# Loading the queries in rows of 2 KB, eight tokens of one head per partition

## The chip, the cores and the metric

The kernel runs on one core of one Trainium2 chip. The metric is the device time of one execution in microseconds (us). The engines are named as in the profile: PE (TensorE matmul) and PEld (its weight loads), DVE (VectorE), ACT (ScalarE), POOL (GpSimd) and SP (SyncE, which issues nearly all DMAs here). A name with a q behind it (SPq, ACTq) is the engine's instruction queue, where DMAs are issued.

## What is computed

Two layers in a row, over B = 4 batches, 768 tokens, 8 heads of 64. First linear attention with a decay per head, in blocks of 64 tokens; then a gated layer whose gate mixes over tokens.

```python
for b in range(nb):                       # 12 blocks of 64 tokens
    intra = einsum('bhic,bhjc->bhij', qb, kb) * Dmask      # lam**(i-j) for i >= j, else 0
    intra = einsum('bhij,bhjd->bhid', intra, vb)
    inter = einsum('bhid,bhde->bhie', qb * lam_pow, kv_state)
    out[:, :, sl] = intra + inter
    kv_state = lam_block * kv_state + einsum('bhsd,bhse->bhde', kb * rev_pow, vb)
x = out as (B, S, H*D)
h = maximum(x @ w_in, 0)
u, v = halves of h;  v_n = (v - mean) / sqrt(var + 1e-6)
v_s = einsum('ts,bsd->btd', w_spatial, v_n) + b_spatial
return (u * v_s) @ w_out
```

## The kernel before

The kernel does not leave the order of its work to a scheduler. The string `ORDER` lists some 700 tokens such as `QM.0.1.D`: a step, its arguments, and the engine that does it (T for PE, D for DVE, A for ACT, P for POOL, S for SP). A loop at the end of the kernel issues each step to its engine in that order. So each engine executes its own tokens strictly in the order of the list, and an instruction that waits holds up all that stand behind it on that engine. Steps of different engines meet only through the data and the buffers that they share.

The attention is done in 12 steps n, three of 256 tokens for each batch. For a step, SP loads k, q and v (`LK`, `LQ`, `LV`, 512 KB each, three buffers of each kind) with 512 bytes in a row: partition p holds the tokens 2p and 2p+1 of all eight heads. `KM` and `QM` (function `decay`, L331; half of the heads in one instruction) multiply k and q by powers of lam, taken from the tables `lv` and `lqn`, into the bf16 tiles `kc` and `qc`. `TK` and `TQ` (L366) transpose these on PE, `EK` and `EQ` evict the transposes into `kT` and `qT`; for some later steps `DK` and `DQ`, transposes by DMA, do the same. `SC` (L396) multiplies them into scores, `MK` (L401) applies the 0/1 mask `m01`, `KP` (L425) builds the state, `AV` adds the state's part (L459) and the block's own part (L468), and `EX` evicts the attention's result, transposed, into `xT`. `VC` and `VD` cast v to bf16.

The second layer follows in the same list: `PV` and `BN` (L493, L508), `PU` (L544), `WT` (transposes of the spatial weights), `PW` (L570), `GP`, `GM` (L576), `PO` (L581), and `ST`, the stores. Weights are loaded by SP (`WH`, `WQ`, `WP`) and cast to bf16 by `CW`, `CX`, `WC`, `WX`.

What matters around the change is the start. Before the first `KM` the two tables must exist. lam is loaded by ACT's queue (`lam`, L200); PE spreads it over 128 partitions by a matmul with a row of ones (`LB`, L216); ACT takes the logarithm (`LN`, L219); DVE multiplies it by the token's position (`LL`, L222, positions from POOL's `posk`, L203 and L204); ACT takes two exponentials (`LX`, L226 and L227), one for each table. Until lam is there, PE executes 13 filler matmuls of a tile of ones (`FL`, L309), which DVE has set to one in its first instruction (`one`, L305). More fillers stand at fixed places in the first third of the list. The start of the list:

```
LK.0.S LQ.0.S LQ.1.S LK.1.S LV.0.S LQ.2.S BR.A lam.A tab.0.A msk.P idn.P posk.P one.D row.D FL.2.256.0.1.T
```

POOL's own first steps are `msk` (L233, L234), `idn` (the identity for transposes), `posk`, and then `QM.1.0` and `QM.1.1`, the query decays of step 1, and `KM.1.0`, `KM.1.1`. DVE's first large steps are `KM.0.0`, `QM.0.0`, `QM.0.1`, `KM.0.1`.

Of the kernel before, what the change touches and what calls it, by code (L numbers as in the profile page):

```python
# [16 lines left out]
LK.0.S LQ.0.S LQ.1.S LK.1.S LV.0.S LQ.2.S BR.A lam.A tab.0.A msk.P idn.P posk.P one.D row.D FL.2.256.0.1.T  # L17
FL.2.256.5.1.T FL.2.256.3.1.T FL.2.256.4.1.T FL.2.256.1.1.T FL.1.256.3.1.T FL.2.256.5.1.T LB.1.T LN.1.A eps.D mkc.D
LL.D LX.A KM.0.0.D QM.0.0.D QM.0.1.D KM.0.1.D FL.1.256.6.1.T BB.1.2.T BB.0.0.T TQ.0.0.3.T FL.2.256.1.1.T TK.0.0.6.T
tab.1.A BE.1.2.A VC.0.A TQ.0.1.4.T TK.0.1.5.T EQ.0.0.3.D EK.0.0.6.D EQ.0.1.4.D EK.0.1.5.D BE.0.0.D FL.1.256.1.1.T  # L20
SC.0.0.2.3.T QM.1.0.P QM.1.1.P KM.1.0.P KM.1.1.P SC.0.1.5.6.T MK.0.0.2.3.D MK.0.1.5.6.D QM.2.1.D FL.2.256.1.1.T
TQ.1.0.1.T FL.4.256.4.1.T TK.1.0.0.T TK.1.1.3.T TQ.1.1.5.T KP.0.2.T AV.0.0.6.4.T QM.2.0.P LK.2.S KM.2.1.P KM.2.0.P
LV.1.S WH.0.S WH.1.S LV.2.S LQ.3.S WH.3.S VD.1.1.P CW.2.P EQ.1.0.1.D SX.0.D EQ.1.1.5.A SY.0.2.A EK.1.1.3.A
FN.0.6.4.D EK.1.0.0.D TQ.2.1.5.T AV.0.1.6.4.T SA.0.1.D EQ.2.1.5.D SC.1.0.1.2.T EX.0.0.6.A EX.0.1.4.A FL.2.256.0.1.T
FL.1.256.3.1.T TQ.2.0.0.T SC.1.1.5.6.T TK.2.1.4.T FL.2.256.3.1.T FL.1.256.3.1.T FL.1.256.3.1.T TK.2.0.3.T
MK.1.0.1.2.D MK.1.1.5.6.D EQ.2.0.0.A VD.1.0.A EK.2.1.4.A KP.1.2.T AV.1.0.0.1.T SY.1.2.D SA.1.0.D FN.1.0.1.D
EK.2.0.3.A SC.2.1.4.5.T FL.1.256.6.1.T CW.0.A CW.1.A SC.2.0.2.3.T AV.1.1.0.1.T WQ.0.S WQ.1.S WQ.2.S WH.2.S WC.0.P
WC.1.P WC.2.P MK.2.1.4.5.D MK.2.0.2.3.D SA.1.1.D VC.2.D CW.3.A EX.1.1.1.A EX.1.0.0.A PV.0.1.6.T PV.0.0.4.T
PV.1.0.5.T KP.2.6.T AV.2.0.2.3.T SA.2.0.D EV.0.1.6.A FN.2.2.3.A EV.0.0.4.A GP.0.0.0.1.A PV.1.1.6.T FL.1.256.0.1.T
AV.2.1.2.3.T EX.2.0.2.A QM.3.1.D QM.3.0.D TQ.3.2.4.T CX.1.D PU.0.1.0.T PU.1.1.2.T EX.2.1.3.A EV.1.1.6.A BN.0.0.D  # L30
EV.1.0.5.A BN.0.1.D RA.0.A EU.0.1.0.A EU.1.1.2.A PV.2.0.3.T PV.2.1.6.T BN.1.1.D BN.1.0.D EV.2.0.3.A RA.1.A
EV.2.1.6.A WT.0.0.3.T WT.2.0.5.T EW.2.0.5.A PU.2.1.2.T WT.1.0.0.T BN.2.0.D RD.1.D BN.2.1.D VN.1.1.D RD.0.D RB.0.D
EW.0.0.3.A RA.2.A VN.0.0.A CX.0.P PU.2.0.6.T EU.2.0.6.A VN.0.1.A EW.1.0.0.D RD.2.D LK.3.S PU.1.0.5.T PU.0.0.3.T
VN.2.0.D VN.1.0.D VN.2.1.D LK.4.S WQ.3.S EU.1.0.5.D GP.0.2.0.6.D EU.2.1.2.A GP.0.1.0.5.A EU.0.0.3.A GP.0.3.0.2.A
KM.3.0.P WQ.4.S WQ.5.S LV.3.S LQ.4.S LQ.5.S LV.4.S KM.4.0.P QM.4.0.P QM.4.1.P QM.5.0.P QM.5.1.P VC.4.P PW.0.0.0.1.T
KM.4.1.D KM.3.1.D WC.3.D GM.0.0.0.1.D PW.0.1.0.5.T PW.0.2.0.6.T TK.3.2.0.T WC.4.A EQ.3.2.4.A EK.3.2.0.A WC.5.D
GM.0.1.0.5.D GM.0.2.0.6.D WT.2.1.3.T WT.0.1.1.T EW.0.1.1.D WP.S VC.3.D EW.2.1.3.A GP.0.1.1.6.A PW.0.3.0.2.T
WT.1.1.4.T LK.5.S GM.0.3.0.2.D SC.3.1.0.1.T KP.3.5.T SC.3.0.2.3.T MK.3.1.0.1.D EW.1.1.4.A PW.0.1.1.6.T TK.4.2.0.T
MK.3.0.2.3.D GP.0.3.1.1.A GP.0.2.1.2.A SY.3.5.A PW.0.3.1.1.T SA.3.1.D SX.3.D GM.0.1.1.6.D GP.0.0.1.3.A TQ.4.2.4.T
PW.0.2.1.2.T GM.0.2.1.2.D GM.0.3.1.1.D PW.0.0.1.3.T GM.0.0.1.3.D EK.4.2.0.A EQ.4.2.4.A KM.5.0.P KM.5.1.P  # L40
AV.3.0.5.6.T SC.4.0.1.2.T KP.4.0.T FN.3.5.6.A AV.3.1.5.6.T SY.4.0.D SC.4.1.3.4.T EX.3.1.6.A TQ.5.2.0.T WX.0.A WX.1.A
EX.3.0.5.D MK.4.0.1.2.D SA.4.1.D MK.4.1.3.4.D SA.4.0.D LV.5.S PV.3.1.6.T PU.3.1.5.T PO.0.1.1.T PO.0.3.2.T TK.5.2.4.T
PV.3.0.3.T LV.6.S LK.6.S EK.5.2.4.D EO.0.1.1.A EQ.5.2.0.A EV.3.1.6.A EU.3.1.5.A EO.0.3.2.D VC.5.P AV.4.0.6.0.T
# [45 lines left out]
def kernel(  # L89
# [37 lines left out]
    ps = psum.tile([P, 8, 512], FP32, name="ps")  # L127
    SB = 7

    lam_in = sb([1, H], FP32, "lam_in")  # L130
    one_row = sb([1, P], FP32, "one_row")
    loglam = sb([P, H], FP32, "loglam")
    ident = sb([P, P], BF16, "ident")
# [186 lines left out]
    def ld_q(e, n):  # L320
        load(q, q_in, n, e)
# [322 lines left out]
```

## Time and profile before

| | |
|---|---|
| time, median of 2 executions | 143.69 us (143.64 to 143.75) |
| the profiled execution: its time, its span | 144.71 us, 143.0 us |
| PE, DVE, ACT, POOL busy, share of the span | 94%, 81%, 58%, 36% |
| granted TensorE clock, mean | 0.972 |
| moved by DMA | 33.60 MB, 235 GB/s over the span |

The page of the profile gives the busy time of each engine, the span in 40 slices, the chain of work that ended last, and the costliest groups of instructions. The timeline lists instructions by start and duration, merged where like ones follow each other ("x2"); a bracket at the end of a row tells how long the engine was idle before and what released it. The windows give the busy time of each engine in a stretch of the span, the clock that TensorE was granted, and the bytes per second of the DMAs. A row is read as: start, duration, engine, line of the kernel, operation, written tile <- read tiles, shapes.

### The profile page before, as it was taken

Reading aid. Unit: us, or ns where it says so; the run is one execution under the profiler, and the core shown is the slowest. Engines: PE = TensorE matmul, PEld = TensorE weight load, DVE = VectorE, ACT = ScalarE, POOL = GpSimd, SP = SyncE. Lnnn points to the kernel's source line nnn. Section 1 sums busy time; section 2 is a strip of 40 time slices with the busy share of each in tenths; the row PEclk is TensorE's granted clock in tenths of the full one; section 3 lists DMA queues with packets and bytes.
Section 4 is the critical chain, followed back from the end, with each engine's and each line's share of the span. In section 5 each row is a group of like instructions: output and inputs, shape, how many; then the busy total and the mean of one; then the engine's idle time right before and its main releaser. Section 6 shows DMA issues by size and latency. Waiting matters only on the chain.

```text
span 143.0 us, 4741 instructions
## 1 busy us (share of the span) xinstructions
PE 133.8 (94%) x1999; PEld 87.7 (61%) x2014; DVE 115.3 (81%) x236; ACT 82.8 (58%) x158; POOL 51.9 (36%) x61
## 2 busy tenths in 40 slices
PE   5969999899999899999999999999999999999990
PEld 4448774676666667567666565676665665666630
DVE  3399798989997769699399988995798889874760
ACT  3422895798978577569611586689113627791121
POOL 5077710555095343991770006920822000000000
PEclk9975899999999999999999999999999999999998
DMA  3999999899999899959904799998994403930284
GB/s 87 347 347 346 386 323 315 294 339 313 337 302 344 259 288 324 285 166 290 293 0 78 49 282 354 180 142 238 276 257 126 177 5 117 406 139 0 78 324 185
DMA packets 54617, 33.60 MB, mean 235 GB/s; under 512 B 11715, under 2 KB 49859, under 8 KB 54596
## 3 DMA queue, kind: packets, MB, share of 16 engines
q1 hardware_dynamic: 54448, 33.17, 80.7%
q8 instruction: 15, 0.25, 0.7%
q10 hardware_dynamic: 148, 0.13, 0.3%
q14 instruction: 6, 0.05, 0.1%
HBM read 24.38 MB, written 6.29 MB: 215 GB/s over the span
## 4 chain that ended last, share of the span: by engine, by line
PE 83%; DVE 9%; ACT 3%; issue 2%; DVEq 0%; ACTq 0%
PE ps L570 21%; PE ps L581 14%; PE ps L493 13%; PE ps L544 11%; PE ps L396 5%; PE ps L366 5%; PE ps L309 4%; PE ps L468 4%; PE ps L425 3%; PE ps L459 2%; DVE st L508 2%; DVE qc L331 2%; DVE kc L331 2%; DVE vn L532 1%; DVE win_sb L183 1%
## 5 line engine op out<-in xcount | busy, mean ns | idle before, releaser
L570 PE MATMUL ps<-wt_sb,vn 128*128 128x384 bf16 x192 | 33.7, 326 | 0.5 <-ACT vn L529 0.3
L331 POOL TENSOR_TENSOR kc<-k_in,lv 128x512 bf16<-128x512 f32 x20 | 20.5, 1043 | 30.0 <-PE ps L493 11.5
L401 DVE TENSOR_TENSOR a_sb<-ps,m 128x1024 bf16<-128x1024 f32 x24 | 28.4, 1211 | 0.7 <-PE ps L425 0.6
L570 PEld LDWEIGHTS <-vn 128*128 128x128 bf16 x192 | 18.3, 98 | 12.3 <-ACT vn L529 0.6
L544 PE MATMUL ps<-xT,win_sb 128*128 128x256 bf16 x192 | 23.6, 273 | 0.5 <-DVE win_sb L183 0.5
L331 POOL TENSOR_TENSOR qc<-q_in,lqn 128x512 bf16<-128x512 f32 x18 | 19.3, 1090 | 10.2 <-DMA q_in<-in_q_dram 5.2
L493 PE MATMUL ps<-win_sb,xT 128*128 128x512 bf16 x89 | 22.3, 379 | 0.4
L581 PE MATMUL ps<-wout_sb,gT 128*128 128x512 bf16 x84 | 22.1, 379 | 0.4
L576 DVE TENSOR_TENSOR gT<-ps,uT 128x384 bf16<-128x384 f32 x32 | 16.8, 551 | 7.1 <-PE ps L570 6.7
L544 PEld LDWEIGHTS <-win_sb 128*128 128x128 bf16 x192 | 18.4, 98 | 5.1 <-DVE win_sb L183 0.7
L181 ACT ACTIVATE ps<-bsp 128x384 f32<-128x384 f32 x23 | 11.2, 490 | 10.7 <-DVE gT L576 6.7
L508 DVE BATCH_NORM_STATS2 st<-vh 128x6 f32<-128x512 bf16 x24 | 16.2, 676 | 1.1 <-ACT vh L498 1.1
L181 ACT ACTIVATE o_sb<-ps 128x512 f32<-128x512 f32 (+1 forms) x14 | 8.0, 579 | 15.4 <-PE ps L581 14.6
L493 PEld LDWEIGHTS <-xT 128*128 128x128 bf16 x96 | 8.8, 98 | 9.6 <-ACT xT L181 0.8
L498 ACT ACTIVATE vh<-ps 128x512 bf16<-128x512 f32 x20 | 11.7, 600 | 4.9 <-PE ps L493 3.2
L181 ACT ACTIVATE xT<-ps 128x512 bf16<-128x512 f32 x20 | 11.0, 598 | 5.8 <-PE ps L468 5.7
L581 PEld LDWEIGHTS <-gT 128*128 128x128 bf16 x92 | 8.7, 98 | 8.6
L498 ACT ACTIVATE uT<-ps 128x512 bf16<-128x512 f32 x20 | 11.7, 590 | 2.0 <-PE ps L544 2.0
L468 PE MATMUL ps<-a_sb,vb 64*64 64x128 bf16 x384 | 10.2, 220 | 0.3 <-issue 0.3
L396 PE MATMUL ps<-qT,kT 64*64 64x128 bf16 x384 | 9.7, 226 | 0.0
L309 PE MATMUL ps<-ones 128*128 128x256 bf16 x32 | 7.5, 368 | 1.6 <-DVE ones L305 1.5
L185 POOL CAST vb<-v_in 128x1024 bf16<-128x1024 f32 (+1 forms) x6 | 5.8, 965 | 7.8 <-PE ps L468 7.8
(79 smaller groups left out, 175.1 us busy)
## 6 DMA issues: line engine op xcount, KB each, us to landing
k_in<-in_k_dram SPq DMA_DIRECT2D x12, 512.0 KB, 6.4
q_in<-in_q_dram SPq DMA_DIRECT2D x12, 512.0 KB, 5.9
v_in<-in_v_dram SPq DMA_DIRECT2D x12, 512.0 KB, 6.1
out_dram<-o_sb SPq DMA_DIRECT2D x23, 256.0 KB, 2.5
wst<-in_moe_w_in_dram SPq DMA_DIRECT2D x4, 512.0 KB, 7.8
wst<-in_moe_w_spatial_dram SPq DMA_DIRECT2D x4, 384.0 KB, 4.5
wst<-in_moe_w_out_dram SPq DMA_DIRECT2D x1, 1024.0 KB, 8.9
wss<-in_moe_w_spatial_dram SPq DMA_DIRECT2D x2, 384.0 KB, 7.7
```

The source lines that it names most:

```text
L181: nc.scalar.activation(out=o, in_=i, func=AF.Copy)
L331: vec(e).tensor_tensor(out=dst[n % NCA][:, u].rearrange("p u m o d -> p o (u m) d"), in0=src[n % NIN].rearrange("p (o u) m d -> p o u m d" ...
L396: nc.tensor.matmul(out=pa[o][row(c), w, j], lhsT=kT[n % NTR][row(o), u, j, c * Q64:(c + 1) * Q64], rhs=qv(n, o, u, c), start=(w == 0 and j ...
L401: nc.vector.tensor_tensor(out=a_sb[n % NA][:, i].rearrange("p o w j x -> p o w (j x)"), in0=ps[:, b0:b1 + 1:b1 - b0].rearrange("p o (w y) ...
L468: nc.tensor.matmul(out=po[c ^ o][row(w), c, i], lhsT=vb[n % NCA][row(c), 4 * o + u, j, :], rhs=a[row(c), i, o, w, j, :], start=(r == 0 and ...
L493: nc.tensor.matmul(out=bank(b), lhsT=x[:, slot(c, g)], rhs=win_sb[:, g, DH:DFF], start=(g == 0), stop=(g == NCH - 1))
L498: nc.scalar.activation(out=o, in_=i, func=AF.Relu)
L508: nc.vector.bn_stats(out=st6[p2][:, t], in_=vh[p2][:, t])
L544: nc.tensor.matmul(out=pu[:, f2].rearrange("p (c x) -> p c x", c=2), lhsT=win_sb[:, g, f * P:(f + 1) * P], rhs=x[:, slot(0, g):slot(1, g) ...
L570: nc.tensor.matmul(out=bank(b)[:, 0:HW], lhsT=vn[bb % 2][:, s, f * P:(f + 1) * P], rhs=wt_sb[:, s, i * HW:(i + 1) * HW], start=False, stop ...
L576: nc.vector.tensor_tensor(out=gT[bb % 2][:, f, cols], in0=bank(b)[:, 0:HW], in1=uT[bb % 2][:, f, cols], op=ALU.mult)
L581: nc.tensor.matmul(out=bank(b), lhsT=gT[bb % 2][:, f, t * P:(t + 1) * P], rhs=wout_sb[:, f, :], start=(f == 0), stop=(f == NCH - 1))
```

## The change

Only the queries' path changes. A step of q is loaded by two DMAs of 256 KB in place of one of 512 KB: heads 0 to 3, then heads 4 to 7. Partition p = 32u + g now holds eight consecutive tokens, 8g to 8g+7, of head u (and of head u+4 in the second half), so that a row is 2 KB. The rest follows that order:

- A partition now belongs to one head, so the table `lqn` needs lam of the partition's own head and a position that runs with p modulo 32. POOL makes the position by a new iota (`posq`), DVE takes it modulo 256 and converts it (`pand`, two instructions), DVE makes a selection matrix from the identity and a diagonal of lam (`sel`, two instructions), `LB` has a second matmul, DVE multiplies in three instructions (`LM`), and the exponential for `lqn` moves behind it as a step of its own (`LY`).
- `QM`, `TQ`, `EQ` handle the same number of elements in as many instructions of the same shapes; their parts are tokens m instead of heads.
- The columns of `qT` that one head's matmuls read (function `qv`, used by `SC` and `AV`) are eight runs of 16 instead of two runs of 64.
- The mask's columns and the eviction `EX` undo the order of the tokens.

In the order list five tokens are new, and no other has moved. The list's start and the stretch that follows the fillers are now:

```
LK.0.S LQ.0.S LQ.1.S LK.1.S LV.0.S LQ.2.S BR.A lam.A tab.0.A msk.P idn.P posk.P posq.P pand.D one.D row.D FL.2.256.0.1.T
...
FL.2.256.5.1.T sel.D LB.1.T LN.1.A eps.D mkc.D LL.D LM.D LX.A LY.A KM.0.0.D QM.0.0.D QM.0.1.D KM.0.1.D FL.1.256.6.1.T
```

```diff
-    mfull = sb([P, 2, 2, P], BF16, "mfull")
-    m01 = sb([P, 2, 2, Q64], BF16, "m01")
+    mfull = sb([P, 2, 8, 32], BF16, "mfull")
+    m01 = sb([P, 2, 8, 16], BF16, "m01")
...
-    lqn = sb([P, NR, H, 2], FP32, "lqn")
+    lqn = sb([P, NR, 2, 8], FP32, "lqn")
...
-        nc.scalar.dma_start(out=lam_in, in_=lam.unsqueeze(0))
+        nc.scalar.dma_start(out=lam_in, in_=lam.rearrange("(o u) -> u o", o=2))
...
+    def c_posq(e):
+        nc.gpsimd.iota(posqi, pattern=[[1, 8]], base=0, channel_multiplier=8)
+
+    def c_pand(e):
+        nc.vector.tensor_single_scalar(out=posqi, in_=posqi, scalar=T2 - 1, op=ALU.bitwise_and)
+        nc.vector.tensor_copy(out=posq, in_=posqi)
+
+    def c_sel(e):
+        nc.vector.tensor_copy(out=sel.rearrange("u (v g) -> u v g", v=4),
+                              in_=ident[0:4, 0:4].unsqueeze(2).broadcast_to((4, 4, 32)))
+        nc.vector.tensor_tensor(out=lam_d, in0=lam_in.unsqueeze(2).broadcast_to((4, 2, 4)),
+                                in1=ident[0:4, 0:4].unsqueeze(1).broadcast_to((4, 2, 4)), op=ALU.mult)
...
-        nc.tensor.matmul(out=bank(b)[:, 0:H], lhsT=one_row, rhs=lam_in, start=True, stop=True)
+        nc.tensor.matmul(out=bank(b)[:, 0:H], lhsT=one_row, rhs=lam_d.rearrange("u o v -> u (o v)"),
+                         start=True, stop=True)
+        nc.tensor.matmul(out=bank(b)[:, H:H + 2], lhsT=sel, rhs=lam_in, start=False, stop=True,
+                         skip_group_check=True)
...
+    def l_m(e):
+        for r in range(NR):
+            nc.vector.scalar_tensor_tensor(out=lqn[:, r], in0=posq.unsqueeze(1).broadcast_to((P, 2, 8)),
+                                           scalar=float(r * T2 - MID),
+                                           in1=loglam[:, H:H + 2].unsqueeze(2).broadcast_to((P, 2, 8)),
+                                           op0=ALU.add, op1=ALU.mult)
+
     def l_x(e):
-        nc.scalar.activation(out=lqn, in_=lv, func=AF.Exp, scale=-1.0)
         nc.scalar.activation(out=lv, in_=lv, func=AF.Exp)
+
+    def l_y(e):
+        nc.scalar.activation(out=lqn, in_=lqn, func=AF.Exp)
...
     def ld_q(e, n):
-        load(q, q_in, n, e)
+        b, t = toks(n)
+        for o in range(2):
+            nc.sync.dma_start(out=q_in[n % NIN][:, o].rearrange("p m d -> p (m d)"),
+                              in_=q[b, 4 * o:4 * o + 4, t].rearrange("u (g m) d -> u g (m d)", m=8))
...
     def q_m(e, n, x):
-        decay(e, qc, q_in, lqn, n, x)
+        w = slice(0, 8) if x == 2 else slice(4 * x, 4 * x + 4)
+        vec(e).tensor_tensor(out=qc[n % NCA][:, w].rearrange("p m o d -> p o m d"), in0=q_in[n % NIN][:, :, w],
+                             in1=lqn[:, n % NR, :, w].unsqueeze(3).broadcast_to((P, 2, w.stop - w.start, D)),
+                             op=ALU.mult)
...
     def qv(n, o, u, c):
-        return qT[n % NTR][row(o), u, :, c * Q64:(c + 1) * Q64]
+        x = 32 * u + 16 * c
+        return qT[n % NTR][row(o), :, x:x + 16]
...
     def e_x(e, n, z, b):
-        copy(e, xT[n % NX][:, z::2].rearrange("p k (y m) -> p k y m", m=2),
-             bank(b).rearrange("p (k m y) -> p k y m", k=NCH, m=2))
+        copy(e, xT[n % NX][:, z::2].rearrange("p k (g m) -> p k g m", m=8),
+             bank(b).rearrange("p (k m g) -> p k g m", k=NCH, m=8))
```

More of the change, by code (lines that the diff above doesn't have):

```diff
@@ L16 @@
 ORDER = """
[L17 to L31, printed above, removed]
@@ L128 @@
     SB = 7
-    lam_in = sb([1, H], FP32, "lam_in")
-    one_row = sb([1, P], FP32, "one_row")
-    loglam = sb([P, H], FP32, "loglam")
+    lam_in = sb([4, 2], FP32, "lam_in")
+    lam_d = sb([4, 2, 4], FP32, "lam_d")
+    sel = sb([4, P], FP32, "sel")
+    one_row = sb([4, P], FP32, "one_row")
+    loglam = sb([P, H + 2], FP32, "loglam")
     ident = sb([P, P], BF16, "ident")
-    mfull = sb([P, 2, 2, P], BF16, "mfull")
-    m01 = sb([P, 2, 2, Q64], BF16, "m01")
+    mfull = sb([P, 2, 8, 32], BF16, "mfull")
+    m01 = sb([P, 2, 8, 16], BF16, "m01")
     posk = sb([P, NR, 2], FP32, "posk")
@@ L294, in b_b @@
     def b_b(e, i, b):
-        nc.tensor.matmul(out=bank(b)[:, 0:HW], lhsT=one_row, rhs=brow[:, i * HW:(i + 1) * HW], start=True, stop=True)
+        nc.tensor.matmul(out=bank(b)[:, 0:HW], lhsT=one_row[0:1], rhs=brow[:, i * HW:(i + 1) * HW], start=True, stop=True)
     def b_e(e, i, b):
@@ L372, in t_q @@
     def t_q(e, n, x, b):
-        tr(n, x, b, qc)
+        for m in range(8) if x == 2 else range(4 * x, 4 * x + 4):
+            nc.tensor.transpose(out=octo(b)[:, m], in_=qc[n % NCA][:, m].rearrange("p o d -> p (o d)"),
+                                identity=ident)
     def e_k(e, n, x, b):
@@ L604, in st_o @@
         eng.dma_start(out=out[bb, t * P:(t + 1) * P, :], in_=o_sb[(bb * NT + t) % NO])
[L606 removed]
+    ops = dict(GT=after, GN=after_vn, one=c_ones, FL=f_l, FX=f_x, WP=w_p, WX=w_x, FN=f_n, lam=c_lam, posk=c_posk, posq=c_posq, pand=c_pand, sel=c_sel, LM=l_m, LY=l_y, tab=c_tab, row=c_row, eps=c_eps, LB=l_b, LN=l_n, LL=l_l, LX=l_x, idn=c_ident, msk=c_mask, mkc=c_mask2, WI=w_in, WS=w_sp, WO=w_out, BR=b_r, BB=b_b, BE=b_e, HL=hold, WH=w_h, CW=c_w, CX=c_x, WQ=w_q, WC=w_c,
                LK=ld_k, LQ=ld_q, LV=ld_v, KM=k_m, QM=q_m, DK=d_k, DQ=d_q, VC=v_c, VD=v_d, TK=t_k, TQ=t_q, EK=e_k, EQ=e_q,
```

82 lines of the change are left out of this document (16 added, 66 removed).

## The prediction

> **What bounds the kernel now.** I read the page first, then busy time by window, then the timeline of the start.
>
> ```profile
> span 143.0 us, 4741 instructions
> PE 133.8 (94%) x1999; PEld 87.7 (61%) x2014; DVE 115.3 (81%) x236; ACT 82.8 (58%) x158; POOL 51.9 (36%) x61
> ...
> 0.00:7.40 7.40, 5.28 (x20) 3.07 (x20) 2.66 (x9) 3.24 (x6) 2.12 (x10) 1.00 0.76 221
> 7.40:16.00 8.60, 7.53 (x137) 5.89 (x141) 7.85 (x14) 2.88 (x5) 6.24 (x6) 0.60 1.14 357
> 16.00:36.40 20.40, 19.18 (x355) 13.63 (x351) 19.23 (x40) 16.64 (x35) 8.53 (x10) 1.00 1.00 322
> 36.40:143.00 106.60, 101.78 (x1500) 65.11 (x1511) 85.51 (x176) 60.07 (x115) 34.97 (x36) 0.99 0.76 209
> ```
>
> The window rows give the stretch, its length, the busy time of PE, PEld, DVE, ACT and POOL, the clock, the DMA share and GB/s. PE's 94% says "bound by PE", but the stages differ. From 36.4 us on PE is busy 101.8 of 106.6 us: whatever time PE enters this stage late is paid in full at the end. Before that, PE's busy time contains fillers, and DVE is as full as PE: 7.85 of 8.60 and 19.23 of 20.40 us. The DMA engines are full too (a share over 1 counts overlapping packets), so I ask whether PE or DVE waits for a transfer there. In the waits, the engines that wait for DMA are mainly ACT and POOL:
>
> ```profile
> ACT vb L181 <- DMA v_in<-in_v_dram: 2.9, 1, 2.9
> POOL wsp_raw L185 <- DMA wst<-in_moe_w_spatial_dram: 5.2, 2, 4.7
> DVE lv L222 <- ACT loglam L219: 2.7, 1, 2.7
> PE ps L366 <- DVE kc L331: 1.0, 1, 1.0
> ```
>
> DVE and PE wait for each other and for the tables (L222, L366), not for loads. So the loads that the change quickens end no wait on the path; the start of the tables is where the path begins:
>
> ```profile
> 0.97 0.48 DVE L305 MEMSET ones<- 128x512 bf16 x1 [0.97 <-PEq L628]
> 1.51 2.96 PE L309 MATMUL ps<-ones 128*128 128x256 bf16 x13 [1.51 <-DVE ones L305]
> 2.50 0.17 POOL L203 IOTA poski<- 128x6 int32 x1
> 2.73 0.19 POOL L204 CAST posk<-poski 128x6 f32<-128x6 int32 x1
> 4.40 0.59 PE L216 MATMUL ps<-lam_in,one_row 1*128 1x8 f32 x2
> 5.03 0.18 ACT L219 ACTIVATE loglam<-ps 128x8 f32<-128x8 f32 x1 [2.15 <-PE ps L216]
> 5.32 0.21 DVE L222 TENSOR_TENSOR lv<-loglam,posk 128x48 f32<-128x48 f32 x1 [2.70 <-ACT loglam L219]
> 5.56 0.24 ACT L226 ACTIVATE lqn<-lv 128x48 f32<-128x48 f32 x1 [0.35 <-DVE lv L222]
> 5.83 0.24 ACT L227 ACTIVATE lv<-lv 128x48 f32<-128x48 f32 x1
> 6.11 0.69 DVE L331 TENSOR_TENSOR kc<-k_in,lv 128x512 bf16<-128x512 f32 x1 [0.58 <-ACT lv L227]
> ```
>
> It is one chain: ones set, 13 fillers, lam's matmul, logarithm, table, exponentials, first decay at 6.11 us.
>
> **The change part by part. (1) The late first instruction of DVE.** `pand` stands ahead of `one` in DVE's order, and its first instruction waits for POOL's new iota, which comes behind `posk`. Behind it on DVE wait the ones; for these waits PE with its 13 fillers; and behind these, in PE's order, stands lam's matmul. `posk` ends at 2.73 + 0.19 = 2.92; an iota of 0.17 ends at 3.09. Two tiny DVE instructions follow, the second of which needs the first. Their nearest row, L222, took 0.21 for 48 columns, these have 8; I take 0.15 each, bounds 0 and 0.21. With 0.05 for the hand-over the ones start at 3.44, not 0.97: **+2.5** (2.1 to 2.6). Nothing hides it, since PE had begun the fillers right behind the ones and lam's matmul right behind the fillers (1.51 + 2.96 = 4.47).
>
> **(2) A second fp32 matmul** in `LB`. The first took 0.59 for two passes, part of which is the latency of the last; a second adds **+0.5** (0.3 to 0.6). `sel` and the mask's copies run on DVE under the fillers and cost nothing, unless lam lands after them; it was there by 4.40, and the fillers now end near 7.0.
>
> **(3) The tables.** `KM.0.0` waited from 5.53 to 6.11 for two exponentials; it now waits for one (0.24), while DVE does the three instructions of `LM`. The same operation on 128x2:
>
> ```profile
> L523 DVE SCALAR_TENSOR_TENSOR nmr<-mv,rstd 128x2 f32<-128x2 f32 x8 | 1.8, 232 | 0.0
> 32.16 0.81 DVE L523 SCALAR_TENSOR_TENSOR nmr<-mv,rstd 128x2 f32<-128x2 f32 x1
> 31.89 1.07 POOL L331 TENSOR_TENSOR kc<-k_in,lv 128x512 bf16<-128x512 f32 x1 [0.99 <-DMA k_in<-in_k_dram]
> ```
>
> One of the eight took 0.81, so the other seven took (1.86 - 0.81)/7 = 0.15; three are 0.45, about the 0.58 that they replace: **0** (-0.3 to +0.1). The exponential of `lqn` follows in 0.3 and is done before `KM.0.0` ends. So `KM.0.0` starts 3.0 late, near 9.1.
>
> **(4) DVE and POOL at once.** [...]
>
> ```profile
> 6.72 1.28 DVE L331 TENSOR_TENSOR qc<-q_in,lqn 128x512 bf16<-128x512 f32 x2
> 7.92 1.55 DVE L331 TENSOR_TENSOR kc<-k_in,lv 128x512 bf16<-128x512 f32 x1
> 7.88 2.49 POOL L331 TENSOR_TENSOR qc<-q_in,lqn 128x512 bf16<-128x512 f32 x2 [4.96 <-ACT bsp L181]
> 9.39 0.41 DVE L183 COPY qT<-ps 128x512 bf16<-128x512 bf16 x1
> ```
>
> Two decays of DVE alone took 1.28, 0.64 each. The fourth, `KM.0.1`, ran beside POOL's `QM.1` and held DVE from 7.92 to 9.39, 1.47: it lost 0.83. Only this one met POOL, because POOL's queries of step 1 came at 7.88 (ACT's bsp, named as releaser, is not what POOL's instruction needs; it is the landing of `LQ.1`). After the change that data lands no later, and POOL waits for `lqn` instead, which is there near 9.4, while `KM.0.0` runs. Three decays of DVE (`QM.0.0`, `QM.0.1`, `KM.0.1`) then run beside POOL's four. Two more at 0.83: **+1.7**. Bounds: DVE always first, -0.8 (the old loss goes too); a whole POOL decay of 1.04 ahead of each of three, 3 x 1.04 - 0.83 = +2.3. I take 1.7, from the one row that shows the pair.
>
> **(5) Does the lag last?** 3.0 + 1.7 = 4.7 at the end of `KM.0.1`. From there EQ, EK, MK and the batch statistics follow on DVE in a fixed order, with 0.75 + 1.17 us idle up to 36.4, and PE's part in between is late with them. The idle time is waiting for PE, not for loads, so it moves along. I take nothing back (at most 1.9). The clock is the exception:
>
> ```profile
> 7.40:8.90 1.50, 1.06 (x14) 0.87 (x14) 1.50 (x2) 0.48 (x1) 1.02 (x2) 0.90 1.15 346
> 8.90:10.30 1.40, 0.77 (x9) 0.47 (x9) 1.40 (x4) 0.00 (x0) 1.40 (x2) 0.50 1.15 349
> 13.00:14.50 1.50, 1.50 (x14) 1.27 (x12) 1.46 (x3) 0.00 (x0) 0.47 (x1) 0.50 1.15 349
> 14.50:16.00 1.50, 1.50 (x65) 1.23 (x68) 0.79 (x3) 1.35 (x3) 0.70 (x1) 0.70 1.08 401
> 34.51 0.33 PE L570 MATMUL ps<-wt_sb,vn 128*128 128x384 bf16 x1
> ```
>
> (the last row, from the timeline, is PE's first matmul of the spatial stage)
>
> PE's gaps between 6.8 and 10.3 are followed by half clock until some 5 us after PE is full again. The new gaps are longer and the same work follows; I take the same length of slow work, 0; bounds are half of the stretch from 8.9 to 14.5 more or less, 2.8 us at half speed, 1.4 either way. [...]
>
> **(6) The loads.** 512 KB at 349 GB/s are 1.50 us; at the 401 GB/s of the window with the weights' 2 KB rows 1.31. So a step of q gains 0.2 us of DMA time. I cost this at nothing on the path: the start's data had landed, and everything that uses it is now later. ACT's 2.9 us wait for v ends before its readers need it. The second DMA a step adds 12 issues to SP, which runs ahead of the data until buffers bind it; 0.
>
> **(7) PE's reads in runs of 16.**
>
> ```profile
> 16.19 0.39 PE L396 MATMUL ps<-qT,kT 64*64 64x128 bf16 x16
> 17.17 0.42 PE L396 MATMUL ps<-qT,kT 64*64 64x128 bf16 x16
> L396 PE MATMUL ps<-qT,kT 64*64 64x128 bf16 x384 | 9.7, 226 | 0.0
> L459 PE MATMUL ps<-qT,s_sb 64*64 64x128 bf16 x160 | 6.2, 223 | 0.0
> L468 PE MATMUL ps<-a_sb,vb 64*64 64x128 bf16 x384 | 10.2, 220 | 0.3 <-issue 0.3
> ```
>
> L396 and L459 read two runs of 64, L468 one of 128, at the same 220 to 226 ns: a break between runs costs nothing that shows. Eight runs are not in the trace. Bounds: 0, or a stream at half speed, which is (0.42 - 0.226)/15 = 13 ns more for each of 544 matmuls, 7.0. I take 0, from the nearest row. The decays, transposes and evictions keep shape and count: 0.
>
> **The sum.** 2.5 + 0.5 + 0 + 1.7 = **+4.7 us**, 144.7 to 149.4 for the profiled execution. That execution lies 1.0 above the median of the runs, so against the median it is 143.7 + 4.7 = **148.4 us** (+3.3%). About 2% is what a measurement of this kernel can tell from no change, so slower begins at 146.6, faster ends at 140.8.
>
> **The rivals.**
>
> *The lag is smaller.* DVE keeps the shared path ahead of POOL at the start, and the old loss goes: 3.0 - 0.8 = 2.2, or a lag of 4.7 of which half is made up before 36.4, 2.35. Time 146.0. For it: POOL's first of the two decays also took long (2.49 for two). Against: POOL will already be waiting when the next decay of DVE comes, and at 7.92 the one that came second lost.
>
> *Not slower: the loads pace the first 36 us.* If the wait that ends last before PE's full stretch at 36.4 is a transfer, a late start vanishes in it, and the six q loads before that point give back 6 x 0.2 = 1.2: 142.5. It decides if DVE or PE is found waiting for a landing between 10 and 36 us. For it: a DMA share of 1.0 to 1.15 throughout. Against: the waits quoted; and weight loads behind `LQ.3` reuse buffers that casts must free, casts which are late as well. [...]
>
> *Short runs slow PE.* All of (7) on top: 148.4 + 7.0 = 155.4. For it only that no row shows such runs.
>
> **How the numbers follow.** Forecast 0.62, with its own range 146.9 (0.5 less contention, 1.0 taken back) to 149.8 (upper bounds of 2, 3 and part of 4); smaller lag 0.25; paced by loads 0.06; short runs 0.06; 0.01 for a gain that I don't see. Slower takes the forecast but 0.02, a quarter of the smaller lag and the short runs: 0.60 + 0.06 + 0.06 = 0.72. Faster 0.03, from gains larger than worked out under the loads' rival and what I don't see; the same 0.25. The range, 145.4 to 150.6, takes in the smaller lag and the upper bounds (1: 2.6, 2: 0.6, 3: 0.1, 4: 2.3, and 1.3 of the clock's 1.4) and leaves out the loads' and the short runs' cases and part of the ends.
>
> **What would show it.** In the changed kernel's timeline: the ones start near 3.4, fillers near 4.0, lam's matmul near 6.9 with four passes, `KM.0.0` near 9.1; `QM.0.0`, `QM.0.1` and `KM.0.1` take about 1.5 each beside POOL; `KM.0.1` ends near 14.2 and PE's first run of L570 comes 4.7 later than 34.5. L396 stays at 226 ns. The prediction is wrong if PE starts before 2 us, if the three decays take 0.65 each, or if the L570 start moves by less than 3 though `KM.0.1` is late.

## The result, and the profile after

The changed kernel takes **183.43 us** (median of 2 executions, 183.17 to 183.68), against 143.69 before: a ratio of **1.271** (95% interval 1.263 to 1.280). The forecast was 148.4 with a range up to 150.6: the direction was right, the size wrong by 35 us. The profiled execution took 183.17 us, with a span of 181.2. Some executions of one kernel run 1.5 to 3% longer than its others: the medians below are those of all its executions, the ratios and their intervals leave the longer ones out, and the profiles of e1 and e3 below are of longer ones.

From the page of the changed kernel, as before: span, busy time, and the rows of PE and of the DMA engines in 40 slices; then the chain that ended last, by engine and by line:

```profile
span 181.2 us, 4776 instructions
PE 143.7 (79%) x2001; PEld 93.0 (51%) x2016; DVE 119.9 (66%) x243; ACT 83.2 (46%) x158; POOL 51.5 (28%) x62
...
PE   1975518985999762999979915999968799999992
...
DMA  4546679899794597866536397697999953094066
...
DMA 36%; PE 36%; SPq 11%; DVE 8%; POOL 3%; issue 3%; ACT 2%; POOLq 0%; DVEq 0%
DMA q_in<-in_q_dram 20%; DMA k_in<-in_k_dram 14%; PE ps L554 8%; PE ps L543 8%; PE ps L517 7%; PE ps L466 6%; SPq L285 6%; SPq L133 5%; DMA qT<-qc 2%; PE ps L369 2%; DVE st L481 2%; PE ps L441 1%; POOL kc L296 1%; POOL qc L307 1%; PE ps L529 1%
```

PE was busy 94% of the span and is now busy 79%; its digits have holes in all thirds of the span. Twenty hundredths of the chain are the queries' transfers, 14 the keys', which did not change themselves but stand in the same queue. And yet the DMA engines are less busy than before: 12 of the 40 digits are a 9, against 23, and the loads' queue takes 67.9% of them, against 80.7%. The transfers are what everything waits for, and yet about a third of the DMA engines' time is free. The windows of the changed kernel (stretch, length, busy time of PE, PEld, DVE, ACT, POOL, clock, DMA share, GB/s) show why:

```profile
4.50:6.00 1.50, 1.50 (x9) 1.06 (x8) 0.53 (x4) 0.00 (x0) 0.00 (x0) 1.00 0.25 91
7.40:16.00 8.60, 7.53 (x61) 4.73 (x61) 5.67 (x14) 2.44 (x5) 0.00 (x0) 1.00 0.70 176
16.00:36.40 20.40, 12.39 (x267) 8.77 (x267) 9.28 (x16) 8.50 (x16) 8.77 (x9) 0.67 0.75 205
36.40:181.20 144.80, 120.50 (x1661) 77.30 (x1674) 103.42 (x206) 71.02 (x137) 40.47 (x42) 0.95 0.70 187
```

While only queries move (4.5 to 6.0 us), the share is 0.25, as of four engines of sixteen, and the rate 91 GB/s. From 7.4 to 36.4 the kernel before moved 357 and 322 GB/s, this one 176 and 205. Who waits: first POOL's wait for queries in the kernel before, then the waits and the timeline of the changed kernel (a row of waits gives the total in us, how often, and the longest):

```profile
POOL qc L331 <- DMA q_in<-in_q_dram: 5.2, 1, 5.2
```

```profile
POOL qc L307 <- DMA q_in<-in_q_dram: 40.0, 6, 14.3
DVE qc L307 <- DMA q_in<-in_q_dram: 13.9, 3, 9.1
3.10 0.17 DVE L147 TENSOR_SCALAR posqi<-posqi 128x8 int32<-128x8 int32 x1 [3.10 <-POOL posqi L144]
3.53 0.48 DVE L267 MEMSET ones<- 128x512 bf16 x1
8.73 0.69 DVE L296 TENSOR_TENSOR kc<-k_in,lv 128x512 bf16<-128x512 f32 x1
11.46 1.29 DVE L307 TENSOR_TENSOR qc<-q_in,lqn 128x512 bf16<-128x512 f32 x2 [2.04 <-DMA q_in<-in_q_dram]
17.33 2.04 POOL L307 TENSOR_TENSOR qc<-q_in,lqn 128x512 bf16<-128x512 f32 x2 [14.26 <-DMA q_in<-in_q_dram]
```

The predicted start is there (ones at 3.53, first decay of the keys at 8.73), but the next instruction waits for the first queries until 11.46, and POOL for those of step 1 until 17.33: one step of 512 KB in 17.33 - 11.46 = **5.87 us**, where 1.5 had been the price. PE's granted clock is 0.67 from 16.0 to 36.4 us, against 1.00 before; what this adds to the waiting was not separated.

The load is written with four heads as the slowest dimension of its source (`u g (m d)`, u of size 4), and 4/16 of 349 GB/s is 87, near the 91 measured; the share of 0.25 agrees. That the size of the slowest dimension sets how many engines carry a load is here a theory of the author's; e1, e2, e7 and e8 try it.

### The profile page after: what moved, and what is told of

Read it like the earlier page. It is cut to its first block, busy times and chain, and to the rows that moved or that the text cites. A ratio compares the mean times of both kernels' runs of the same rounds, so it can differ in the third digit from the quotient of the medians.

```text
span 181.2 us, 4776 instructions
## 1 busy us (share of the span) xinstructions
PE 143.7 (79%) x2001; PEld 93.0 (51%) x2016; DVE 119.9 (66%) x243; ACT 83.2 (46%) x158; POOL 51.5 (28%) x62
## 3 DMA queue, kind: packets, MB, share of 16 engines
q1 hardware_dynamic: 45136, 33.17, 67.9%
## 4 chain that ended last, share of the span: by engine, by line
DMA 36%; PE 36%; SPq 11%; DVE 8%; POOL 3%; issue 3%; ACT 2%; POOLq 0%; DVEq 0%
DMA q_in<-in_q_dram 20%; DMA k_in<-in_k_dram 14%; PE ps L554 8%; PE ps L543 8%; PE ps L517 7%; PE ps L466 6%; SPq L285 6%; SPq L133 5%; DMA qT<-qc 2%; PE ps L369 2%; DVE st L481 2%; PE ps L441 1%; POOL kc L296 1%; POOL qc L307 1%; PE ps L529 1%
## 5 line engine op out<-in xcount | busy, mean ns | idle before, releaser
L517 PE MATMUL ps<-xT,win_sb 128*128 128x256 bf16 x192 | 25.0, 283 | 0.0
L554 PE MATMUL ps<-wout_sb,gT 128*128 128x512 bf16 x84 | 23.2, 395 | 0.6 <-issue 0.2
L517 PEld LDWEIGHTS <-win_sb 128*128 128x128 bf16 x192 | 19.0, 101 | 5.2 <-DVE win_sb L120 0.2
L344 PE MATMUL ps<-ident,qc 128*128 128x128 bf16 x56 | 6.6, 266 | 13.1 <-DVE qc L307 7.9
L398 PE MATMUL ps<-vb,kc 64*64 64x64 bf16 x320 | 6.1, 211 | 10.5 <-POOL vb L122 10.5
L307 DVE TENSOR_TENSOR qc<-q_in,lqn 128x512 bf16<-128x512 f32 x6 | 4.9, 840 | 13.9 <-DMA q_in<-in_q_dram 13.9
L344 PEld LDWEIGHTS <-qc 128*128 128x128 bf16 x56 | 4.6, 120 | 16.1 <-DVE qc L307 9.5
```

Of the source, the lines that this page charges most:

```text
L307: vec(e).tensor_tensor(out=qc[n % NCA][:, w].rearrange("p m o d -> p o m d"), in0=q_in[n % NIN][:, :, w], in1=lqn[:, n % NR, :, w].unsquee ...
L344: nc.tensor.transpose(out=octo(b)[:, m], in_=qc[n % NCA][:, m].rearrange("p o d -> p (o d)"), identity=ident)
L517: nc.tensor.matmul(out=pu[:, f2].rearrange("p (c x) -> p c x", c=2), lhsT=win_sb[:, g, f * P:(f + 1) * P], rhs=x[:, slot(0, g):slot(1, g) ...
L554: nc.tensor.matmul(out=bank(b), lhsT=gT[bb % 2][:, f, t * P:(t + 1) * P], rhs=wout_sb[:, f, :], start=(f == 0), stop=(f == NCH - 1))
```

## Experiments

In a kernel called "permuted", the queries arrive with heads and tokens in another order, so that its result is not the reference's and its time alone is of use; its instructions are those of its counterpart. Ratios are against the kernel before on the same chip, with 95% intervals. The notes on record name the runs by the first part of their label (e1 is e1_rows32).

### The load: e1, e2, e3, e4, e7, e8

```diff
 e1 (in the changed kernel; permuted)
-  in_=q[b, 4 * o:4 * o + 4, t].rearrange("u (g m) d -> u g (m d)", m=8)
+  in_=q[b, 4 * o:4 * o + 4, t].rearrange("u (g m) d -> g u (m d)", m=8)
 e2 (in the changed kernel; permuted; half = the o-th 128 tokens of the step)
+  in_=q[b, :, half].rearrange("h (g m) d -> h g (m d)", m=8)
 e3 (in the changed kernel: eight DMAs of 64 KB a step)
+  for u in range(4):
+    nc.sync.dma_start(out=q_in[n % NIN][32 * u:32 * u + 32, o]..., in_=q[b, 4 * o + u, t].rearrange("(g m) d -> g (m d)", m=8))
 e4 (in the kernel before: rows of 512 B, heads 0 to 3, then 4 to 7)
+  nc.sync.dma_start(out=q_in[n % NIN][:, 4 * o:4 * o + 4]..., in_=q[b, 4 * o:4 * o + 4, t].rearrange("h (p m) d -> p h (m d)", m=2))
 e7 (in the kernel before: the changed kernel's load alone; permuted)
+  in_=q[b, 4 * o:4 * o + 4, t].rearrange("u (g m) d -> u g (m d)", m=8)
 e8 (as e7 with e1's "g u (m d)"; permuted)
```

> One word differs from the changed kernel: the source of a query load is walked with the 32 row groups outermost and the 4 heads inside them, instead of the heads outermost. Two DMAs of 256 KB in rows of 2 KB as there; the rows come to other partitions, so the values are those of a permuted order of the queries. Theory A (a DMA whose outermost dimension has 4 entries runs on 4 of the 16 DMA engines: 512 KB of queries at a quarter of 349 GB/s take 5.9 us): with 32 outermost all 16 are used, the query loads take 1.3 to 1.5 us, and what is left is the late start, 147 to 150 us. Rival B (2 KB rows, or eight tokens to a partition, are slow in themselves): 183 us. Rival C (two DMAs a step hold up SP's queue): 183 us.

> The changed kernel with each query DMA taking all 8 heads of half the tokens, heads outermost: the outermost dimension has 8 entries, rows of 2 KB, two DMAs of 256 KB; the queries come in a permuted order. Theory A: 8 of 16 DMA engines, a step of queries takes 2.9 us in place of 5.9, 12 steps 35 us on these engines in place of 70; the start is hardly later than its own 2.6 us lag, but the loads of steps 4 to 11 lag some: 150 to 160 us. Rivals B and C: 183 us.

> The changed kernel with one DMA for each head, eight of 64 KB a step, each of 32 partitions by 2 KB; the same data at the same places as the changed kernel, so its output is the reference's. Theory A: 32 rows outermost, all 16 engines, 147 to 151 us, if 84 more issues on SP at some 0.5 us each do not come in the way. Rival C (number of DMAs): slower than 183 us. Rival B: 183 us.

> The kernel before with its query load cut in two DMAs of four heads each, rows of 512 bytes and the 128 partitions outermost as before. Nothing else of the change. Theory A: 143.2 to 144.5 us. Rival C (two DMAs a step are what costs): clearly slower, 150 to 183 us. Rival B says nothing against 143.7.

> The kernel before with nothing but the changed kernel's query load: two DMAs of 4 heads each, heads outermost, 2 KB to a partition; the tile is read in the old order, so the queries are permuted. Theory A (4 of 16 DMA engines, and this alone makes the changed kernel slow): 177 to 184 us. Rival (the new order of the tokens in decays, transposes and matmuls makes 10 us or more of the 40): 150 to 173 us.

> The kernel before with the load of run e1_rows32: rows of 2 KB, 32 row groups outermost, two DMAs a step; permuted queries. It gives what rows of 2 KB are worth by themselves. The prediction's step 6 (512 KB in 1.3 us in place of 1.5, but off the path): 143 to 144.5 us beside a kernel before of 143.7 to 145, that is 0 to 1% less. If the rows of 512 bytes were no limit (e1_rows32 showed 346 to 358 GB/s where the kernel before showed 349): the same as the kernel of run e4_two512.

Measured: e1 149.37 us, **1.027** (1.021 to 1.033). e2 156.94, 1.073 (1.068 to 1.078). e3 167.11 (median of 4, 162.84 to 167.60; no ratio). e4 144.41, 0.993 (0.989 to 0.996). e7 177.97, **1.231** (1.226 to 1.237). e8 145.27, **1.000** (0.996 to 1.005). The same window while only queries move, in e1 and in e2, then SP's queries and a later window of e3:

```profile
4.50:6.00 1.50, 1.50 (x9) 1.04 (x8) 0.53 (x4) 0.00 (x0) 0.00 (x0) 1.00 1.02 346
```

```profile
4.50:6.00 1.50, 1.50 (x9) 1.07 (x8) 0.53 (x4) 0.00 (x0) 0.00 (x0) 1.00 0.54 187
```

```profile
1.32 8.76 SPq L286 DMA_DIRECT2D q_in<-in_q_dram  x16
9.00:12.00 3.00, 3.00 (x11) 1.47 (x10) 2.51 (x5) 1.74 (x2) 0.20 (x1) 1.00 0.44 127
```

Slowest dimension 4, 8, 32: shares 0.25, 0.54, 1.02 and 91, 187, 346 GB/s. With no byte and no row changed but the order in which the source is walked, 34 us are gone in e1. e7 puts the four-headed load alone into the kernel before: 33 us. So the load is the cause, both ways. The packets of 2 KB themselves are no slower: of those that start between 4.5 and 6.0 us the median took 84 ns in the changed kernel and 85 in e1, but at most 6 are under way at once in the one, and 20 in the other. e8 prices what the change was made of, rows of 2 KB, at a share of 1.10 and 342 GB/s from 7.4 to 16.0 us: nothing. e3, far above its expectation, met another limit: its slowest dimension is 32, and yet the share is 0.44 from 9 to 12 us. SP issued one DMA per 8.76/16 = 0.55 us, and 64 KB in 0.55 us are 120 GB/s, about the 127 of that window.

### The start: e5, e6, e9, e10, e12

```diff
 e5 (on e1), e12 (on the changed kernel), part of e9
- ... posk.P posq.P pand.D one.D row.D FL ... sel.D LB.1.T
+ ... posk.P posq.P one.D row.D FL ... pand.D sel.D LB.1.T
...
 e6 (on e1), e10 (on the kernel before): a copy on POOL that reads the result of KM.0.1
- ... QM.1.0.P QM.1.1.P
+ ... GK.P QM.1.0.P QM.1.1.P
+ nc.gpsimd.tensor_copy(out=seen, in_=kc[0][0:1, 3, 1, 1, 0:1])
 e9 (changed kernel, p = 4g + u: e1's order of the source and the reference's result; positions, sel and e5's edit not shown)
...
+  in_=q[b, 4 * o:4 * o + 4, t].rearrange("u (g m) d -> g u (m d)", m=8)
+  return qT[n % NTR][row(o)].rearrange("p m (g u) -> p m g u", u=4)[:, :, 16 * c:16 * c + 16, u]
```

> The kernel of run e1_rows32 (queries in a permuted order, 16 DMA engines) with two tokens moved: pand stands behind one and row, just ahead of sel, so DVE sets the ones first again. If the prediction's steps hold (2.5 us for the late ones, and two more decays slowed beside POOL because the tables are late): the fillers start at 1.5, KM.0.0 at 6.2 to 6.4, and only KM.0.1 meets POOL; 3.5 to 4.5 us less than e1_rows32, 0.3 to 1 above the kernel before. Rival (only the direct lag of 2.5 counts, the rest of e1_rows32's 4.3 lies elsewhere, in the reads in runs of 16 or in the second stage): 2 to 2.7 less than e1_rows32.

> The kernel of run e1_rows32 with one small POOL instruction ahead of QM.1.0 that reads one element of what KM.0.1 writes, so that POOL's decays begin only behind DVE's. If DVE's decays lost 2.4 us beside POOL in e1_rows32 and this lasts to the end: QM.0.0 to KM.0.1 take 0.65 each, KM.0.1 ends near 11.4 in place of 13.8, and the time is 1.5 to 2.4 below e1_rows32 (POOL's own decays are 2 us later, which may take part back). Rival (the slowed decays cost nothing in the end, POOL's queries of step 1 are needed as soon): same as e1_rows32 or up to 2 above.

> A whole kernel with rows of 2 KB on 16 DMA engines: partition p = 4g + u in place of 32u + g, so that the queries' source can be walked with the 32 row groups outermost and every value is where the computation wants it; positions, selection matrix and the columns that one head reads (16 at a step of 4) follow. pand stands behind the ones as in e5_ones_first. If reads of TensorE at a step of 8 bytes are as free as the runs of 16 were: the time of e5_ones_first, 1.2 to 2.0% above the kernel before. Rival (strided reads slow the stream): 544 matmuls at up to 13 ns more, up to 7 us above e5_ones_first.

> The kernel before with one small POOL instruction ahead of QM.1.0 that reads an element of what KM.0.1 writes, as in e6_pool_waits: DVE's fourth decay no longer meets POOL's first. If the 0.83 us that KM.0.1 lost in the profile lasts to the end: 0.5 to 0.9 us below the kernel before. Run e4_two512, where POOL's data landed 0.18 us later and KM.0.1 took 0.69, was 0.75% below. Rival (POOL's decays, 1.5 us later, are needed by PE): same or slower.

> The changed kernel itself, on the chip of the other runs of this group. If the 5 us between its 183.4 us and the 178.0 us of run e7_load4 come from the rest of the change: 1.26 to 1.28 of the kernel before. If they lie between chips: near 1.23.

> The changed kernel with its 4-engine loads, and pand moved behind the ones. In the changed kernel's profile QM.0.0 waited for its queries until 11.5, well behind the tables at 8.9. If the late start is hidden there: the same as e11_changed_again within 0.5 us. If it still counts: 2 us or more less.

Measured: e5 147.36, 1.018 (1.013 to 1.023). e6 147.71, 1.021 (1.016 to 1.026). e9 152.25, 1.054 (1.047 to 1.061). e10 145.98, 1.008 (1.005 to 1.012). e11 183.34, 1.267 (1.258 to 1.276). e12 183.62, 1.270 (1.260 to 1.279). The start of DVE in e1, then in e6:

```profile
8.72 0.69 DVE L296 TENSOR_TENSOR kc<-k_in,lv 128x512 bf16<-128x512 f32 x1
9.33 2.98 DVE L307 TENSOR_TENSOR qc<-q_in,lqn 128x512 bf16<-128x512 f32 x2
12.23 1.53 DVE L296 TENSOR_TENSOR kc<-k_in,lv 128x512 bf16<-128x512 f32 x1
```

```profile
9.34 1.29 DVE L310 TENSOR_TENSOR qc<-q_in,lqn 128x512 bf16<-128x512 f32 x2
10.54 0.69 DVE L299 TENSOR_TENSOR kc<-k_in,lv 128x512 bf16<-128x512 f32 x1
```

In e1 the three decays beside POOL's took 2.98/2 = 1.49 and 1.53 each, as predicted; in e6, where POOL waits, 0.64 and 0.69. But either cure gained less than its lag: of e1's 2.7%, e5 leaves 1.8 and e6 2.1, gains that are little more than the intervals. In e10 the kernel before lost 0.8% by it, though there too `KM.0.1` fell from 1.55 to 0.68 us: the delay of POOL's decays of step 1 costs more than DVE gains. So e6, and later e15 and e17, may pay for this copy as well. Under the changed kernel's own load the late start costs nothing (e12 against e11), where the first query decay waits for its data in any case.

e9 computes the reference with quick loads (share 1.16 and 315 GB/s from 7.4 to 16.0 us, against 0.70 and 176 in the changed kernel), and pays for it in PE. Its scores (L370) and state products (L433), then those of e1:

```profile
L370 PE MATMUL ps<-qT,kT 64*64 64x128 bf16 x384 | 14.4, 284 | 0.0
L433 PE MATMUL ps<-qT,s_sb 64*64 64x128 bf16 x160 | 8.3, 283 | 0.0
```

```profile
L369 PE MATMUL ps<-qT,kT 64*64 64x128 bf16 x384 | 9.6, 226 | 0.2 <-DVE qT L120 0.2
L432 PE MATMUL ps<-qT,s_sb 64*64 64x128 bf16 x160 | 6.2, 223 | 0.0
```

Runs of 16 neighbours cost nothing (226 and 223 ns, as before the change); every fourth element makes a matmul 58 to 60 ns longer. As matmuls overlap, PE's busy time grows by less: 14.4 + 8.3 - 9.6 - 6.2 = 6.9 us in all, 13 ns for each of the 544. The time is 4.9 us above that of e5, which has the same order of the start.

### What was left: e13 to e18

The load alone made 1.231, the whole change 1.267 to 1.271. The 5 us between them were no part of any theory so far, and e7 had run on another chip than the changed kernel. e13 and e14 put both on one chip; e15 takes the late ones and the decays beside POOL away at once.

```diff
 e13 = e7 again, e14 = the changed kernel again; e15 = e1 with the edits of both e5 and e6
```

> The kernel before with nothing changed but the changed kernel's query load (queries arrive permuted, so that its result is that of permuted queries), this time on the same chip as the changed kernel. Theory (the chip's four-engine transfers differ in speed, the rest of the change costs nothing under the slow load): within 1.5 us of e14, so 182 to 184. Rival (the rest of the change costs some 5 us under the slow load too): 177 to 179 again, 4 to 6 below e14.

> The changed kernel as it is, beside the load alone on one chip. Theory (chip): 178 to 184, within 1.5 us of e13. Rival (the rest of the change): 183, 4 to 6 above e13.

> The changed kernel with the source walked 32 outermost (permuted queries), the ones set ahead of pand, and POOL waiting for KM.0.1: both prices of the start taken away at once, on sixteen DMA engines. Theory (the two prices add, and what the change costs beside its load is the start alone): 145.3 to 146.5, within 0.9 of the kernel before plus the second matmul's 0.5. Rival (the two overlap, or something else in the change costs too): 147.0 to 147.6, as with either alone.

Measured: e13 178.13, 1.235 (1.225 to 1.245). e14 183.53, 1.270 (1.260 to 1.281). e15 146.96, 1.019 (1.011 to 1.027). The theory fell twice: the 5 us belong to the change and not to the chip, and e15 is no better than e5 or e6 alone. Part of that may be its copy on POOL, which cost 0.8% in e10. The 5 us, though, need something else in the change that costs time. The rows of the DMA queue (packets, MB, share of 16 engines' span) of e13 (span 177.8 us) and e14 (181.7):

```profile
q1 hardware_dynamic: 45136, 33.17, 66.2%
```

```profile
q1 hardware_dynamic: 45136, 33.17, 67.3%
```

The same packets and bytes took 0.662 x 177.8 = 117.7 us of each engine in e13 and 0.673 x 181.7 = 122.3 in e14. The trace has each packet's duration; those of 512 bytes, which are k, v and (in the kernel before) q:

| kernel | mean ns | up to 27 ns | 28 to 38 ns | longer |
|---|---|---|---|---|
| before | 27.8 | 99% | 0% | 1% |
| e8 | 28.0 | 99% | 0% | 1% |
| e13 | 29.3 | 90% | 4% | 6% |
| e14 | 31.8 | 71% | 14% | 14% |
| e15 | 30.4 | 56% | 41% | 3% |

So k's and v's rows, which nobody touched, are slower wherever the change's tiles are declared. No trace has the tiles' addresses; what follows is the author's count of the declared sizes, each taken, by assumption, as rounded up to 32 bytes. The change adds `sel` (512 bytes a partition), `lam_d`, `posqi` and `posq` (32 each), and makes `loglam` 32 larger: 640 bytes, all ahead of the large tiles. In the kernel before, the tiles up to and with `gap`, an unused tile of 120 numbers, and the four constants that the program sets first come to 4096 bytes by this count, a multiple of 512. The change leaves `gap` alone, and 640 = 512 + 128: every load of k, v and q should now land 128 bytes past such a multiple.

```diff
 e16 (the changed kernel), e17 (e15)
-    gap = sb([P, 120], FP32, "gap")
+    gap = sb([P, 88], FP32, "gap")
 e18 (the kernel before)
-    gap = sb([P, 120], FP32, "gap")
+    gap = sb([P, 152], FP32, "gap")
```

> The changed kernel with nothing but its unused padding tile cut from 120 to 88 numbers, so that all large SBUF tiles start at a multiple of 512 bytes again, as they do in the kernel before; the change's new small tiles had moved them to 128 bytes past one. Theory (misplaced tiles make DMA packets longer, which is the 5.4 us between the load alone and the whole change): 177.5 to 179.5, packets of 512 bytes back at a mean of 29 ns instead of 32, few of them at 31 to 36. Rival (the rest of the change costs it in another way): 182.5 to 184.

> e15 (source walked 32 outermost, queries permuted; ones first; POOL waits for KM.0.1) with the padding tile cut in the same way. Theory: 1 to 2 below e15, so 145.0 to 146.0, about the kernel before and its second matmul. Rival: 147, as e15.

> The kernel before with nothing but its unused padding tile grown from 120 to 152 numbers, so that its large tiles start 128 bytes past a multiple of 512, as in the changed kernel. Theory: slower by 1 to 2 us, 1.007 to 1.015, with packets of 512 bytes at a mean of some 30 ns instead of 27.8. Rival (place is of no matter): 1.000 within 0.004.

Measured: e16 178.92, **1.240** (1.231 to 1.249). e17 146.48, 1.010 (1.004 to 1.016). e18 147.27, **1.019** (1.013 to 1.024). The medians of e17 and e18 lie a little above what was expected. Packets of 512 bytes: 29.3 ns and 4% between 28 and 38 in e16, 27.7 and 0% in e17, 31.4 and 55% in e18. The windows of e18, to be held against the two of the kernel before that the prediction shows, then its main wait for a load and the start of PE's full stretch; below them the same wait in the kernel before:

```profile
7.40:16.00 8.60, 8.33 (x155) 6.37 (x157) 7.69 (x16) 2.90 (x5) 5.58 (x5) 1.00 1.20 290
16.00:36.40 20.40, 17.67 (x330) 12.13 (x320) 16.30 (x35) 14.71 (x30) 9.13 (x10) 1.00 1.07 333
POOL kc L331 <- DMA k_in<-in_k_dram: 22.0, 5, 11.0
37.33 2.93 PE L570 MATMUL ps<-wt_sb,vn 128*128 128x384 bf16 x17
```

```profile
POOL kc L331 <- DMA k_in<-in_k_dram: 7.9, 3, 6.6
```

In the first window the share is higher than before (1.20 against 1.14) and the rate lower (290 against 357 GB/s): busier engines, fewer bytes. The second window makes some of it up (333 against 322); over both, 8.60 x (357 - 290) - 20.40 x (333 - 322) = 352 KB fewer have arrived by 36.4 us. PE enters its full stretch (L570) at 37.33 instead of 34.51. That is 2.8 us, about the 2.7 of the result, but this start alone does not set the time: in e8 it came at 35.7, at the time of the kernel before. e16 against e14 and e11 removes the shift alone from the changed kernel, and 4.6 and 4.4 us go with it; what remains, 1.240, is the load alone (1.231 and 1.235) within the intervals.

How the place makes a packet longer is not shown. Most of the longer packets of e18 lie at 31 to 36 ns, and no run shows why 40% of its packets kept their 27. So the place is shown as a cause by e16, e17 and e18; a mechanism is not.

## Why the prediction was wrong, by its steps

**Step 6, the loads, failed,** in size and in sign. It priced a step of queries by its bytes and its rows, at 401 GB/s, as a gain of 0.2 us that nobody waits for. It measured 5.87 us instead of 1.50. The step looked at the length of the rows and not at the order in which the source's dimensions are walked, which the diff showed (`u g (m d)`). Of the 1.271, this alone makes 1.231 to 1.235. The reading that loads end no wait on the path was narrow as well: it went by DVE and PE, and of POOL's waits for transfers it named only one for weights (5.2 us), not the 7.9 for k and the 5.2 for q in the same trace. When loads grew slower in e18, these waits grew, to 22.0 and 13.2. A smaller premise failed too: rows of 2 KB ran at 346 GB/s (e1), no faster than the 349 with 512 bytes, and were worth nothing (e8: 1.000). The 401 GB/s was the rate of one window of 1.5 us; over the 20.4 us from 16.0 to 36.4 e8 moved 363 GB/s and e17 360.

**A term was missing: where the tiles lie.** No step had it: the diff's new tiles were counted by the instructions on them (steps 1 to 3), never by the bytes that they add. So more than the queries' path changed: the loads of k and v changed with it. In the kernel before the shift costs 1.9% (e18); under the slow load it makes the step from 1.240 to 1.270.

**"The loads pace the first 36 us"** was a rival at 0.06, for a gain. Its condition held (DVE waited for queries until 11.46 and again until 26.86 us, 2.0 and 9.1 long), with the other sign: a load that nobody waits for is hidden only as long as it keeps its price.

**Steps 1 to 4 were right in place and in most sizes.** The ones began at 3.53 (forecast 3.44). `KM.0.0` began at 8.73 (near 9.1), 2.6 late rather than 3.0: the tables gained 0.35, a little over their bound. The forecast's inner range up to 149.8 does not follow from the bounds it names, which add 0.8 to 148.4 at most; the wider range, to 150.6, does. With a quick load the decays beside POOL took 1.5 each, as forecast (0.64 and 0.69 in e6, where POOL waits; what the two engines contend for, no run shows), and `KM.0.1` ended at 13.76 (e1; forecast 14.2); in the changed kernel they don't meet, since DVE and POOL each wait for queries, and e12 shows that nothing of the late start reaches the end.

**Step 5, "I take nothing back", failed where it could be tried.** e1 is the change with the load mended, and at 2.7% it seems to confirm the forecast's 3.3%. It does so for another reason in part: mending the start leaves 1.8% (e5) or 1.9% (e15), and mending start and placement (e17) 1.0%. What e5 leaves is about what the shift alone costs (1.9% in e18). So the lag was worth some 0.8 or 0.9% of 145, about 1.2 us at the end (the intervals allow 0 to 2.5). The traces agree: `KM.0.1` ends at 13.76 in e1 and at 9.09 in e15, 4.7 us sooner, but PE's first matmul of the spatial stage comes at 39.4 and 37.9, 1.5 sooner. So some 3 us of the lag were gone by then; that they went into waits for loads that the shift had made slower is likely, but not shown. What the lag would cost with the tiles in place was not run.

**Step 7 was right:** runs of 16 cost nothing (226 and 223 ns in e1, as before the change). The upper bound of 7.0 us for broken reads was about the price of the strided ones in e9 (6.9 us of PE's busy time).

What stays open is, first, the last 1.0% of e17. It still has the copy on POOL, which by itself cost the kernel before 0.8% (e10), and the second matmul of `LB`, which starts 0.45 us behind the first; no run has start and places mended without the copy, so the copy may be most of it. Open are also pauses of PE with nothing to wait for. They come with the slow load (9.3 us in e7, 1.7 in e1, at the line of `KP`); these rows are the waits of the changed kernel, then of e16:

```profile
PEld L398 <- issue: 12.0, 6, 5.8
```

```profile
PEld L398 <- issue: 9.7, 6, 4.6
```

What PE waits for there was not tried. The only version below the kernel before is e4, two transfers of 512-byte rows, at 0.993: less than the 2% that count.

## What to carry to other kernels

Read a DMA's access pattern from its slowest dimension inwards before pricing its bytes: the query loads here ran at 91 GB/s with a slowest dimension of 4, at 187 with 8 and at 346 with 32, and a transfer that was off the path at the full rate was the path at a quarter of it. A change that adds small tiles can move the large ones declared behind them; compare their places. Here a move by 512 bytes in all left nothing beside the load's own cost (e16), and one of 128 cost 1.9% (e18). And when a mended version lands on the forecast, still take the forecast's own terms away one by one: e1 agreed in the sum with terms that were not the cause.

## What the runs showed of the hardware that was not expected

- The rate of the query loads went with the size of the slowest dimension of their source: 91 GB/s for 4, 187 for 8, 346 for 32.
- Large tiles moved by 128 bytes made loads of 512-byte rows slower: 290 instead of 357 GB/s from 7.4 to 16.0 us, 31.4 instead of 27.8 ns a packet, 1.9% of the kernel (e18).
- Rows of 2 KB and of 512 bytes ran at the same rate, where the slowest dimension is 32 or 128 (346 against 349 GB/s).
- SP's queue put out 16 DMAs of 64 KB in 8.76 us, one per 0.55 us (e3).
- PE's moving operand in runs of 16 bf16 costs nothing (226 ns for 128 columns); at every fourth element the same matmul takes 284, and 13 ns more of PE's busy time.
